# Tap rows among the first fillers, and a filter transpose that hands half of its PSUM banks to the first filter stage

## The chip, the cores and the metric

The kernel runs on one core of one Trainium2 chip. The metric is device time in microseconds for one execution of the whole program; for a set of runs, the median. TensorE, VectorE (DVE), ScalarE (ACT), GpSimd (POOL) and SyncE (SP) each run their own list of instructions in order and wait for each other on semaphores. Transfers are issued from SP and from GpSimd and run on 16 DMA engines.

## What is computed

One block of a sequence model with S = 2048 positions, D = 448 channels and F = 1792 hidden units, all in bfloat16. A mixer part and a part that mixes along the sequence follow each other, each with a layer norm ahead and a residual behind:

```python
k_shift = sum over t of k_pad[:, t:t + S, :] * shift_k[:, ks - 1 - t]   # ks = 4 taps
kv = k_shift * v
y  = irfft(rfft(kv, 2S) * rfft(ssm_k, 2S))[:, :S, :] + kv * ssm_D       # long convolution
h  = x + layernorm(x) * y
u  = gelu(einsum("bsd,sf->bdf", layernorm(layernorm(h)), w1) + b1)
h2 = h + transpose(einsum("bdf,fs->bds", u, w2) + b2)
```

Here x is the input q. The filter ssm_k is D x S: channels come first in memory, so it has to be transposed before it can be treated like kv.

## The kernel before

The sequence is laid out as 128 partitions times R = 16 rows: position 16 q + r is partition q, row r. All work is on rows of 448 channels.

The long convolution is a Fourier transform in two stages, made with matmuls. The first stage multiplies each of the 16 rows by a table E of sines (two matmuls a row, into two PSUM banks), ScalarE copies the pair of banks to a ring in SBUF (L943), and two transfers shuffle it to the layout of the second stage: the larger part from GpSimd's queue, the smaller from SP's (both L947). The ring (`wring`) has 8 buffers, so the copy of a row waits until the shuffle eight rows earlier has landed. The second stage (L964) takes the block table FW. Both stages run once for the filter ("k1", "k2") and once for kv ("u1", "u2"). Products of the two spectra (L1015) and a first inverse stage (L1027) follow, a shuffle back (L1037), a second inverse stage (L1103) with the gate and the statistics of the two layer norms, and then three long runs of matmuls: L1198 and L1208 with w1, L1218 with w2.

Ahead of that stand:

- the loads (`emit_loads`), all on SP's queue: the filter in four blocks of channels (L808, the 64-channel one first), ssm_D (L828), the taps shift_k in one partition (L811), k and v in four pieces each (L816, L825), and last the three rows of k that each partition needs from its neighbour, the halo (L820, L822)
- the tables (`emit_tables`): E from sines on ScalarE (L764), FW and the inverse tables through a chain over GpSimd, VectorE and ScalarE (L771, L775, L777, L779, L788, L791); the table set of the activation functions is changed once (L793)
- the taps (`emit_kv`): a matmul with a row of ones spreads each of the four tap rows to all partitions (L868), and a copy brings it to SBUF. Then, for each row, VectorE multiplies four shifted rows of k by the taps (L879), TensorE adds the four products with an identity (L885), and VectorE multiplies two rows of the sum by v (L888). u1 needs the result
- the filter transpose (`emit_kT`): 64 transposes (L914), for each of 8 groups of two rows and each of 4 blocks of channels, into PSUM, and one copy to SBUF a group
- fillers (`dummy`, L904): matmuls without use, 9 at the start and 3 after some transposes

A copy out of PSUM is written once (`evac`) and goes to ScalarE (L652, with a scale L653) or VectorE (L655, with a scale L656).

The order is not written by hand. Every operation gets a due time `sch.t0`; a list scheduler (`schedule`) takes, for each engine, among the operations that are ready by its cost estimates and that can get their PSUM banks or ring buffers, the one with the earliest due time. The result is a fixed list of instructions for each engine with the waits that the data and the buffers demand. PSUM has 8 banks, given out by the scheduler at the first write and taken back after the last read. The constants T_... and N_... at the top of the build are the due times and the numbers of fillers.

Of the kernel before, what the change touches and what calls it, by code (L numbers as in the profile page):

```python
# [509 lines left out]
def _build(nc, A_q, A_k, A_v, A_shift_k, A_ssm_k, A_ssm_D, B_w1, B_b1, B_w2, B_b2, out):  # L510
# [35 lines left out]
    o_SK = o_WT + 3584  # L546
# [19 lines left out]
    with ctx:  # L566
# [69 lines left out]
            return PS[:, b.slots[i], :].bitcast(dt_)  # L636

        FX = ("act", "dve")
        T_KV, T_DKV, T_KT, T_K1, T_DK1, T_U1, T_DU1 = -37.75, 0.96, -26.42, -39.56, 0.44, 2.72, 0.9
        T_K2, T_U2, T_D2, T_CT, T_BIAS, T_I1, T_DI1 = 29.29, -14.6, 1.375, 22.37, 56.3, 7.01, 0.974  # L640
        T_Q, T_DQ, T_I2, T_DI2, T_M1, T_W1 = 83.98, 14.35, 85.76, 0.401, 102.98, 122.45

        T_TH, T_TN = -36.0, -30.0
        T_CP, T_XL, T_WB = 20.0, -35.53, 154.44
        N_WZ, N_WI, N_W0, N_WK = 34, 6, 9, 3

        def evac(dst, src, w, b, n, scale=None, engs=FX, r=(), est=None):

# [155 lines left out]
        def emit_loads():  # L804
            Dq = "sp"
            for i, c in enumerate((3, 0, 1, 2)):
                sch.t0 = -20.0 + i
                op(Dq, lambda e, W, c=c: e.dma_start(KN[0:CW[c], c, :], A_ssm_k[128 * c:128 * c + CW[c], :]),  # L808
                   w=[(o_KN + 4096 * c, 4096)], dmab=CW[c] * 4096)
            sch.t0 = -15.0  # L810
            op(Dq, lambda e, W: e.dma_start(SK[0:1, :], A_shift_k.rearrange("(a d) j -> a (d j)", a=1)),  # L811
               w=[(o_SK, 3584)], dmab=3584, keng=1)
            op("pool", lambda e, W: e.memset(KH[0:1, 0:3, :], 0.0), w=[(o_KH, 3 * DB, "halo")], n=3 * D)
            for c in range(4):
                sch.t0 = -14.0 + c
                op(Dq, lambda e, W, c=c: e.dma_start(KH[:, 3 + 4 * c:7 + 4 * c, :], k2d[:, 4 * c:4 * c + 4, :]),  # L816
                   w=[(o_KH + (3 + 4 * c) * DB, 4 * DB)], dmab=128 * 4 * DB)
                if c == 3:
                    sch.t0 = -10.5
                    op(Dq, lambda e, W: e.dma_start(KH[1:113, 0:3, :], k2d[0:112, 13:16, :]),  # L820
                       w=[(o_KH, 3 * DB, "halo")], dmab=112 * 3 * DB)
                    op(Dq, lambda e, W: e.dma_start(KH[113:128, 0:3, :], k2d[112:127, 13:16, :]),  # L822
                       w=[(o_KH, 3 * DB, "halo")], dmab=15 * 3 * DB, keng=15)
# [37 lines left out]
        ONE = view(o_one, [128])  # L861

        def emit_kv():
            sch.t0 = -39.0
            op("pool", lambda e, W: e.memset(ONE, 1.0), w=[(o_one, 256)], n=128)
            for j in range(4):
                b = _Buf(psum)
                op("pe", lambda e, W, b=b, j=j: e.matmul(  # L868
                    Pb(b), ONE[0:1, :], SK[0:1, :].rearrange("p (d j) -> p j d", j=4)[:, 3 - j, :], start=True, stop=True),
                   r=[(o_one, 256), (o_SK, 3584)], bw=[b], n=D)  # L870
                evac(lambda j=j: WT[:, j, :], lambda b=b: Pb(b), [(o_WT + j * DB, DB)], b, D)
            for c in range(8):
                sch.t0 = T_KV + T_DKV * c
# [32 lines left out]

        def emit_kT():
            bs = [_Buf(psum) for _ in range(8)]
            for i, c in enumerate((3, 0, 1, 2)):
                for g in range(8):  # L910
                    sch.t0 = T_KT + 0.9 * g
                    for rr in range(2):
                        r = 2 * g + rr
                        k = op("pe", lambda e, W, b=bs[g], rr=rr, r=r, c=c: e.transpose(  # L914
                            out=Pbf(b, 0)[:, rr * D + 128 * c:rr * D + 128 * c + CW[c]],
                            in_=KN[0:CW[c], c, r:S:R], identity=ID[0:CW[c], 0:CW[c]]),
                            r=[(o_KN + 4096 * c, 4096), (o_ID, 256)], bw=[bs[g]], kind="tr")
                    if g == 5 and i < 3:
                        dummy(N_WK, T_KT + 0.9 * g, (k,))
            for g in range(8):  # L920
                sch.t0 = T_KT + 0.9 * g
                evac(lambda g=g: KT[:, 2 * g:2 * g + 2, :].rearrange("p a d -> p (a d)"),
                     lambda b=bs[g]: Pbf(b, 0)[:, 0:2 * D], [(o_KT + 2 * g * DB, 2 * DB)], bs[g], 2 * D,
                     est={"act": 911.0, "dve": 630.0})
# [353 lines left out]
```

## Time and profile before

| | us |
|---|---|
| median of 13 runs | 191.87 |
| lowest and highest run | 189.38, 192.84 |
| the profiled execution | 189.38 |
| its span, first to last instruction | 187.6 |
| busy: TensorE, VectorE, ScalarE, GpSimd | 172.7, 109.3, 97.2, 73.5 |
| first L943 copy starts | 16.47 |
| last inverse shuffle (GpSimd, L1037) is issued | 82.29 |

The span leaves out 1.8 us of the execution around the instructions. A busy TensorE is not TensorE at its peak, and fillers count as busy. The views used below are the page (busy shares in 40 slices and the costliest groups), the chain of waits that ended last, the timeline of one engine (start, duration, engine, line, operation, shapes, count; in brackets the idle time of the engine before it and what ended it), busy time by stretches, and the answers on single lines of the source with the time from a transfer's issue to its landing.

### The profile page before, as it was taken

The page shows a single profiled execution, that of the slowest core. Times are in us where ns is not written, and L with a number is a line of the kernel's source. Part 1 is how long each engine was busy: PE and PEld are TensorE (multiplying, and loading weights), DVE is VectorE, ACT ScalarE, POOL GpSimd, SP SyncE. Part 2 cuts the span into 40 slices and gives each one's busy share as a digit, 9 for nine tenths or more (in the row PEclk, how much of TensorE's full clock was granted, in tenths as well). Part 3 has the DMA queues.
Part 4 walks back from the last instruction along what each step waited for, and adds up shares of the span by engine and source line. Part 5 has one row for each costly group of instructions (what it writes and reads, how often), then busy time and mean ns, then how long its engine had stood idle before and what let it go on. Part 6 is the DMA issues. An engine that isn't in the chain of part 4 may idle for free.

```text
span 187.6 us, 2810 instructions
## 1 busy us (share of the span) xinstructions
PE 172.7 (92%) x1025; PEld 91.2 (49%) x1025; DVE 109.3 (58%) x179; ACT 97.2 (52%) x141; POOL 73.5 (39%) x178
## 2 busy tenths in 40 slices
PE   7998898999997989899599599999999999999993
PEld 2644343434332433244245245455556777777772
DVE  8859799797789999996877874100000222212221
ACT  3487989979889989932984285262121000000000
POOL 8935987698710044485488755100000000000000
PEclk9999999999999999999999999999999999999999
DMA  5998698788649997773999997000000100111111
GB/s 160 365 417 311 171 236 241 211 239 233 193 148 345 388 372 234 223 218 111 380 419 418 414 404 301 7 0 0 0 0 3 49 19 30 49 49 52 49 49 49
DMA packets 15725, 35.44 MB, mean 189 GB/s; under 512 B 3869, under 2 KB 9886, under 8 KB 15710
## 3 DMA queue, kind: packets, MB, share of 16 engines
q1 hardware_dynamic: 11102, 25.59, 36.5%
q0 software_dynamic: 4608, 9.66, 18.0%
q8 instruction: 8, 0.13, 0.3%
q14 instruction: 7, 0.06, 0.1%
HBM read 22.37 MB, written 1.84 MB: 129 GB/s over the span
## 4 chain that ended last, share of the span: by engine, by line
PE 62%; POOL 11%; DMA 9%; ACT 8%; DVE 5%; issue 3%; SPq 1%; POOLq 0%; ACTq 0%
PE ps L1218 23%; PE ps L1208 11%; PE ps L1198 7%; DMA arena<-arena 6%; PE ps L1027 5%; ACT arena L652 4%; PE ps L964 4%; DMA arena<-in_A_ssm_k_dram 3%; PE ps L885 3%; POOL arena L947 3%; PE ps L933 3%; POOL arena L1152 2%; PE ps L914 2%; PE ps L1103 1%; POOL arena L1149 1%
## 5 line engine op out<-in xcount | busy, mean ns | idle before, releaser
L1222 DVE SCALAR_TENSOR_TENSOR arena<-ps,arena 128x448 bf16<-128x448 f32 x16 | 10.9, 684 | 55.2 <-PE ps L1218 55.2
L1218 PE MATMUL ps<-arena 128*128 128x448 bf16 x224 | 42.5, 353 | 0.0
L1218 PEld LDWEIGHTS ps<-arena 128*128 128x128 bf16 x224 | 32.3, 144 | 10.1
L943 ACT CAST arena<-ps 128x896 bf16<-128x896 f32 x32 | 26.7, 931 | 3.5 <-PE ps L937 1.4
L1198 PE MATMUL ps<-arena 128*128 128x448 bf16 x112 | 23.0, 353 | 1.0 <-DVE arena L1158 1.0
L652 ACT CAST arena<-ps 128x896 bf16<-128x896 f32 (+1 forms) x26 | 22.0, 909 | 3.5 <-PE ps L868 2.6
L947 POOL DMA_DIRECT2D arena<-arena x32 | 19.2, 602 | 6.1 <-ACT arena L943 3.4
L1208 PE MATMUL ps<-arena 128*128 128x448 bf16 x112 | 21.5, 353 | 0.0
L964 PE MATMUL ps<-arena 128*64 128x448 bf16 x128 | 16.4, 362 | 1.8 <-ACT arena L652 1.0
L1110 ACT ACTIVATE arena<-ps,arena 128x448 f32<-128x448 f32 x16 | 11.1, 724 | 13.2 <-PE ps L1103 8.5
L1037 POOL DMA_DIRECT2D arena<-arena x16 | 9.4, 594 | 20.8 <-PE ps L964 15.6
L1188 ACT ACTIVATE arena<-ps,arena 128x448 bf16<-128x448 f32 x14 | 8.1, 642 | 18.0 <-PE ps L1208 14.3
L879 DVE TENSOR_TENSOR arena<-arena 128x1792 bf16<-128x1792 bf16 x16 | 17.4, 1122 | 0.0
L933 PE MATMUL ps<-arena 128*128 128x448 bf16 x64 | 16.0, 355 | 1.3 <-ACT arena L943 1.3
L1198 PEld LDWEIGHTS ps<-arena 128*128 128x128 bf16 x112 | 10.9, 98 | 11.7 <-DVE arena L1158 2.0
L1015 DVE TENSOR_TENSOR arena<-arena 128x1792 bf16<-128x1792 bf16 x16 | 16.4, 1085 | 0.0
L1208 PEld LDWEIGHTS ps<-arena 128*128 128x128 bf16 x112 | 11.0, 98 | 10.2
L885 PE MATMUL ps<-arena 128*128 128x448 bf16 x64 | 14.5, 354 | 1.5 <-ACT arena L943 1.4
L1027 PE MATMUL ps<-arena 64*128 64x448 bf16 x128 | 14.1, 352 | 1.3 <-DVE arena L1015 0.6
L1117 DVE SCALAR_TENSOR_TENSOR arena<-arena 128x448 f32<-128x448 bf16 x16 | 10.5, 679 | 4.7 <-ACT arena L1110 4.6
L655 DVE CAST arena<-ps 128x896 bf16<-128x896 f32 (+2 forms) x11 | 9.5, 876 | 2.7 <-PE ps L868 1.2
L964 PEld LDWEIGHTS ps<-arena 128*64 128x64 f16 x128 | 5.4, 108 | 11.4 <-ACT arena L652 4.6
(86 smaller groups left out, 199.1 us busy)
## 6 DMA issues: line engine op xcount, KB each, us to landing
arena<-arena POOLq DMA_DIRECT2D x48, 196.0 KB, 5.7
arena<-in_B_w_dram SPq DMA_DIRECT2D x8, 896.0 KB, 15.4
arena<-in_B_w_dram SPq DMA_DIRECT2D x2, 2048.0 KB, 9.6
arena<-in_B_w_dram SPq DMA_DIRECT2D x2, 1536.0 KB, 17.0
arena<-in_A_k_dram SPq DMA_DIRECT2D x4, 448.0 KB, 8.7
arena<-in_A_v_dram SPq DMA_DIRECT2D x4, 448.0 KB, 9.0
arena<-in_A_q_dram SPq DMA_DIRECT2D x4, 448.0 KB, 5.9
out_dram<-arena SPq DMA_DIRECT2D x7, 224.0 KB, 1.9
```

What stands on the lines that cost most here:

```text
L652: return e.copy(out=dst(), in_=src())
L879: op("dve", lambda e, W, T=T, i=i, r=r: e.tensor_tensor(out=T[:, i], in0=KH[:, r:r + 4, :], in1=WT, op=ALU.mult), r=[(o_KH + r * DB, 4 * D ...
L885: op("pe", lambda e, W, b=b, T=T, i=i, j=j: e.matmul(Pb(b, i), ID, T[:, i, j, :], start=(j == 0), stop=(j == 3)), r=[(o_ID, 256), (o + (i ...
L933: op("pe", lambda e, W, b=b, r=r, h=h, dl=dl: e.matmul(Pb(b, h), E[:, 2 * r + h, :], src[:, r, :], start=True, stop=not dl), r=[r_E(r), (o ...
L943: return e.copy(out=dst, in_=Ppair(b)) if W == "act" else e.tensor_copy(out=dst, in_=Ppair(b))
L947: shuf[tag + q_ + str(r)] = shuf[tag + q_] = op(q_, lambda e, W, w=w, p0=p0, a=a, b_=b_, j0=j0: e.dma_start(T[p0:p0 + 29:4, j0:j0 + (b_ - ...
L964: op("pe", lambda e, W, b=bs[h], h=h, j=j, c=c, par=par: e.matmul(PS[64 * par:64 * par + 64, b.slots[c], 0:D], FW[:, 64 * c:64 * c + 64], ...
L1015: op("dve", lambda e, W, m=m, i=i: e.tensor_tensor(out=MR(m.slots[0]).rearrange("p (x y) d -> p x y d", x=2), in0=TU[:, i].unsqueeze(2).br ...
L1027: k = op("pe", lambda e, W, b=bs[h], m=ms[h], par=par, t=t, tab=tab, xy=xy, P=P: e.matmul(Pb(b, par), tab[P, :], MR(m.slots[0])[P, xy, :], ...
L1198: op("pe", lambda e, W, r=r, fc=fc, b=bs[fc]: e.matmul(Pb(b), W1A[:, r, 128 * fc:128 * fc + 128], Q[:, r, :], start=(r == 0), stop=(r == R ...
L1208: op("pe", lambda e, W, r=r, fc=fc, b=b: e.matmul(Pb(b), W1B[:, r, 128 * (fc - n0):128 * (fc - n0) + 128], Q[:, r, :], start=(r == 0), sto ...
L1218: op("pe", lambda e, W, r=r, fc=fc, b=b: e.matmul(Pb(b), W2[fc // 7][:, fc % 7, r:S:R], G[:, fc, :], start=(fc == 0), stop=(fc == NFC - 1) ...
```

## The change

Four things are edited, all of the opening:

1. The taps' load gets an earlier due time (-25 instead of -15), so that it is the first transfer on SP. The four matmuls that spread the taps get a due time of -62 instead of -39 and an estimate of their own; they come among the fillers that open TensorE's list.
2. The filter transpose walks its groups in two halves. Groups 0 to 3 are transposed block by block as before, as each block of the filter arrives. Groups 4 to 7 follow group by group, with due times between those of the first filter stage, so that four banks are free for that stage before they begin.
3. The first filter stage gets due times that start later and lie further apart.
4. Constants: the due times of u2 and of the products, and fewer fillers (8 instead of 9 at the start, 2 instead of 3 behind transposes).

```diff
-        T_KV, T_DKV, T_KT, T_K1, T_DK1, T_U1, T_DU1 = -37.75, 0.96, -26.42, -39.56, 0.44, 2.72, 0.9
-        T_K2, T_U2, T_D2, T_CT, T_BIAS, T_I1, T_DI1 = 29.29, -14.6, 1.375, 22.37, 56.3, 7.01, 0.974
+        T_KV, T_DKV, T_KT, T_K1, T_DK1, T_U1, T_DU1 = -37.75, 0.96, -45.0, -25.62, 0.72, 2.72, 0.9
+        T_K2, T_U2, T_D2, T_CT, T_BIAS, T_I1, T_DI1 = 29.29, -15.87, 1.375, 22.37, 56.3, -30.85, 0.584
...
-        N_WZ, N_WI, N_W0, N_WK = 34, 6, 9, 3
+        N_WZ, N_WI, N_W0, N_WK = 34, 6, 8, 2
...
-            sch.t0 = -15.0
+            sch.t0 = -25.0
             op(Dq, lambda e, W: e.dma_start(SK[0:1, :], A_shift_k.rearrange("(a d) j -> a (d j)", a=1)),
...
         def emit_kv():
-            sch.t0 = -39.0
+            sch.t0 = -62.0
...
-                   r=[(o_one, 256), (o_SK, 3584)], bw=[b], n=D)
+                   r=[(o_one, 256), (o_SK, 3584)], bw=[b], n=D, est=380.0)
...
             bs = [_Buf(psum) for _ in range(8)]
-            for i, c in enumerate((3, 0, 1, 2)):
-                for g in range(8):
-                    sch.t0 = T_KT + 0.9 * g
-                    for rr in range(2):
-                        r = 2 * g + rr
-                        k = op("pe", lambda e, W, b=bs[g], rr=rr, r=r, c=c: e.transpose(
...
-                    if g == 5 and i < 3:
-                        dummy(N_WK, T_KT + 0.9 * g, (k,))
+            order = [(c, g) for c in (3, 0, 1, 2) for g in range(4)] + [(c, g) for g in range(4, 8) for c in (3, 0, 1, 2)]
+            t_g = [T_KT + 0.9 * g if g < 4 else T_K1 + T_DK1 * (2 * g - 5) for g in range(8)]
+            for i, (c, g) in enumerate(order):
+                sch.t0 = t_g[g]
+                for rr in range(2):
+                    r = 2 * g + rr
+                    k = op("pe", lambda e, W, b=bs[g], rr=rr, r=r, c=c: e.transpose(
...
+                if i in (3, 7, 11):
+                    dummy(N_WK, T_KT + 0.9 * g, (k,))
             for g in range(8):
-                sch.t0 = T_KT + 0.9 * g
+                sch.t0 = t_g[g]
```

What the scheduler makes of it, by the lists of instructions: TensorE's list has 1021 matmuls instead of 1025. It begins with 7 fillers, the four tap matmuls and one more filler. ScalarE copies all four tap rows ahead of the sines. The first row of the first filter stage stands ahead of the last transposes. In GpSimd's list the first shuffle moves ahead of L771. From the middle of the first inverse stage on, the lists of all engines are the same as before. Lines after the change's diff move down by one (L943 becomes L944, and so on); the text before the result uses the numbers of the kernel before.

More of the change, by code (lines that the diff above doesn't have):

```diff
@@ L908, in emit_kT @@
             bs = [_Buf(psum) for _ in range(8)]
-            for i, c in enumerate((3, 0, 1, 2)):
-                for g in range(8):
-                    sch.t0 = T_KT + 0.9 * g
-                    for rr in range(2):
-                        r = 2 * g + rr
[L914 to L917, printed above, removed]
-                    if g == 5 and i < 3:
-                        dummy(N_WK, T_KT + 0.9 * g, (k,))
+            order = [(c, g) for c in (3, 0, 1, 2) for g in range(4)] + [(c, g) for g in range(4, 8) for c in (3, 0, 1, 2)]
[5 more added lines that the diff above has]
+                    k = op("pe", lambda e, W, b=bs[g], rr=rr, r=r, c=c: e.transpose(
+                        out=Pbf(b, 0)[:, rr * D + 128 * c:rr * D + 128 * c + CW[c]],
+                        in_=KN[0:CW[c], c, r:S:R], identity=ID[0:CW[c], 0:CW[c]]),
+                        r=[(o_KN + 4096 * c, 4096), (o_ID, 256)], bw=[bs[g]], kind="tr")
+                if i in (3, 7, 11):
+                    dummy(N_WK, T_KT + 0.9 * g, (k,))
             for g in range(8):
-                sch.t0 = T_KT + 0.9 * g
+                sch.t0 = t_g[g]
                 evac(lambda g=g: KT[:, 2 * g:2 * g + 2, :].rearrange("p a d -> p (a d)"),
```

## The prediction

> **What bounds the kernel now.** I read the chain of waits first, for what sets the end, then the timelines of ScalarE, VectorE, GpSimd and the SP queue over the opening, then busy time by stretch, then single lines for their transfers.
>
> The chain (start, duration, what):
>
> ```profile
> 1.99 5.97 DMA arena<-in_A_ssm_k_dram
> ...
> 13.39 1.53 PE ps L914 x16
> ...
> 16.47 0.91 ACT arena L943
> ...
> 30.98 0.53 ACT L793
> ...
> 33.28 0.93 PE ps L885 x4
> ...
> 82.93 4.56 DMA arena<-arena
> ...
> 142.32 42.39 PE ps L1218 x224
> ```
>
> The end hangs on a TensorE run that is back to back from about 107 to 184.7 us. What feeds it begins with the last shuffle of the inverse (82.93), and that hangs, through two long stages of copies, on the opening: filter load, transposes (L914), first ScalarE copy at 16.47. So a change of the opening counts only as far as it moves 82.93.
>
> ScalarE and VectorE after the opening (start, duration, count, idle before and its releaser):
>
> ```profile
> 16.47 8.19 ACT L943 CAST arena<-ps 128x896 bf16<-128x896 f32 x10 [1.37 <-PE ps L937]
> 30.94 1.28 ACT L793 ACT_TABLE_LOAD   x1
> ...
> 19.89 3.09 DVE L879 TENSOR_TENSOR arena<-arena 128x1792 bf16<-128x1792 bf16 x3
> 36.05 1.09 DVE L888 TENSOR_TENSOR arena<-ps,arena 128x896 bf16<-128x896 f32 x1 [1.12 <-PE ps L885]
> 46.19 1.09 DVE L888 TENSOR_TENSOR arena<-ps,arena 128x896 bf16<-128x896 f32 x1 [0.86 <-PE ps L885]
> ```
>
> VectorE runs the kv chain (15 of 16 L879, all 8 L888) from 19.89 to 47.28: 27.4 us, with four gaps that sum to 2.7 us (0.23, 1.12, 0.53, 0.86). ScalarE copies at 0.80 us start to start beside it.
>
> ```profile
> 12.00:16.50 4.50, 4.50 (x34) 2.48 (x34) 3.69 (x10) 3.13 (x6) 0.52 (x2) 1.00 1.02 416
> 19.90:33.30 13.40, 11.45 (x57) 4.93 (x58) 13.14 (x14) 12.76 (x17) 10.77 (x20) 1.00 0.82 226
> 50.00:80.00 30.00, 26.88 (x240) 10.19 (x238) 27.83 (x28) 27.93 (x34) 9.07 (x20) 1.00 0.82 277
> ```
>
> Columns: stretch, length, busy PE, PEld, DVE, ACT, POOL, clock, DMA share, GB/s. The k and v loads fill the DMA engines before 16.5 (share 1.02). From 19.9 to 33.3 VectorE and ScalarE are both nearly full, and again from 50 to 80.
>
> Why VectorE starts at 19.89:
>
> ```profile
> 8.07 0.45 SPq L820 DMA_DIRECT2D arena<-in_A_k_dram  x1
> ...
> L822 SPq DMA_DIRECT2D arena<-in_A_k_dram x1: 440/440/440, 8.6 to 8.6; - x1
> ...
> DMA to landing us min/median/max: 10.9/10.9/10.9
> ```
>
> The halo rows of k (L820, L822), last in the queue of loads, land at 8.56 + 10.9 = 19.5, and the second L879 in VectorE's order needs them.
>
> **What the Trainium skill says.** "DMA: Bandwidth & Descriptors", section "Queues, rings and completion order": each DMA engine serves the queues in turn, packet by packet, and takes one queue's descriptors in ring order. The trace agrees on the order: the tap load, 3.5 KB, issued at 3.31, was only waited for and met at 9.49, behind the filter blocks. No long stretch of the trace has shuffles against loads, so the sharing is not shown. "TensorE: Matmul & The Clock Gate", Part 1: the array runs at half rate at first and again after an idle window of about 3.4 us. The trace shows the first: nine fillers in 3.54 us, 0.37 us apart, against 0.19 later. "ScalarE: Activation LUTs", "What ACT_TABLE_LOAD costs": about 1283 ns; the trace has 1.28 us.
>
> **The change part by part.**
>
> *Tap load first on SP, taps among the fillers.* L811 takes 0.22 us plus 0.04 on SP, so the four filter loads are issued, and land, 0.26 later; all loads after its old place keep their issue time, but in a full queue they land 0.26 later too. In an empty queue the taps land by 0.73 + 3.6 = 4.3 at the latest (3.6: the first filter load, issue to landing). TensorE has run its 7 fillers by 1.38 + 7 x 0.37 = 4.0, so the taps take about 4.1 to 6.1 (4 x 0.48), where TensorE had nothing else: cost zero. ScalarE now copies all four taps (0.43 each) ahead of the sine tables L764, which start at 6.4 instead of 5.32; the GpSimd copies behind them (L985) end about 1.1 later, covered by GpSimd's idle 4.8 us before L771. If that cover were gone, L771 would move by the 1.1.
>
> *Four fillers fewer* (one of 9, three of 9): 4 x 0.19 to 0.37 us on an engine that waits for loads: zero.
>
> *Transposes.* 64 before and after. Groups 0 to 3 hold four banks; the fourth filter block lands at about 9.3 + 0.26 = 9.5, eight transposes at 0.1 follow, 10.3; VectorE copies (0.53 each; it does seven of the eight, five before, and no taps, all ahead of its wait for the halo), 10.9; row 0 of the first stage on TensorE from 11.1; ScalarE, in its order behind two more pieces of L764 and one copy, starts L943 at 12.2 instead of 16.47: **4.3 us earlier**.
>
> *What is late next.* The L943 copies write a ring of 8 buffers. The ninth waits until the first shuffle out of the ring has landed, its GpSimd part and its SP part. The SP part stands behind all k, v and halo loads in SP's queue. So ScalarE makes eight copies, 12.2 to about 20.6, and stops until the halo has landed. In that wait it also does L779 (0.80) and the table load with its activation (1.4), which the order puts after the sixth and seventh copy.
>
> *What the early shuffles do to the loads.* In GpSimd's new order one shuffle is issued at 13.4, the second behind L771 (16.0), the third and fourth behind L775 (17.5 and 18.1); then L788 and L791 wait for L779 and hold the fifth until 21.8. Four shuffles of 196 KB fall among the loads. Price of one: at least 200.7 KB at 416 GB/s, 0.48 us; at most at the rate of the stage that is nearly all shuffles, 226 GB/s at share 0.82, so 276 GB/s when busy, 0.73 us. I take 0.70, near the top, since the loads have no slack and shuffles move poorly. The halo lands at 19.5 + 0.26 + 4 x 0.70 = 22.5 and VectorE restarts at 22.6: **2.7 us later** (2.2 to 3.2 between the bounds).
>
> *The balance.* At its restart VectorE has 2.7 us less time; ScalarE has more behind it: 8 copies instead of 4.3 by 19.89 (3.7 x 0.80 = 3.0), L779 and the table load (2.2): 5.2 us. From there to the end of the inverse the two engines share the copies out of PSUM (L652/L655, L653/L656), so at best 5.2/2 = 2.6 us comes back; not all, since the kv chain is VectorE's alone and L943 ScalarE's alone. The least that comes back is the gap at 36.05 (1.12, which the chain leads back to the table load) and, by estimate, 0.4 of the other three: 1.5. I take 2.25. Sum: 2.7 - 2.25 = **+0.45 us** (-0.4 at 2.2 less 2.6, +1.7 at 3.2 less 1.5).
>
> *After that* the order of instructions is unchanged: the last 568 on TensorE, 89 on VectorE, 51 on ScalarE are the same in both. The product stage's new due times only reorder u2, k2 and products inside the full stretch, 50 to 80: zero, within 0.4 either way. The shift passes to the end one to one.
>
> Against the profiled execution: 189.38 + 0.45, span 187.6 to 188.05. That execution is the quickest of the runs shown; against the median of 191.87 I get 192.3.
>
> **The rivals.**
>
> *Traded away* (0.60): as above, 192.3. For: DMA share 1.02 while the loads run; the ring.
>
> *Loads starve* (0.20), slower. If the halo's last packets are not in by about 23, when the fifth shuffle starts to move (issued 21.8), the shuffles of four more full buffers go ahead too: 8 x 0.70 instead of 4 x 0.70, halo at 25.3, VectorE 5.5 us late, 5.5 - 2.25 = +3.2: 195.1. TensorE would then stand idle near 3.4 us before L885 and might fall to half rate. For: the margin is half a microsecond. Against: ScalarE's stop itself ends the supply of shuffles.
>
> *Early start kept* (0.12), faster. If loads keep the engines and shuffles take only the leavings, the halo lands near 19.5 + 0.26 + 0.2, VectorE is 0.4 late, and 0.4 - 2.25 = -1.9: 190.0. Against: packets are served in turn, and nothing orders a load first.
>
> *It doesn't start earlier* (0.08). If the taps still wait, or cold fillers push the transposes, L943 starts near 15: two shuffles fall among the loads (+1.4 + 0.26), about 1.6 us of ScalarE work plus 0.8 comes ahead: 1.66 - 1.2, rounded +0.4: 192.3 as well.
>
> **How the numbers follow.** A measurement of this kernel tells about 1% from no change, 1.9 us. Slower by more: the starved case and the upper tail of the first, 0.24. Faster by more: most of the third case and a little of the others, 0.13. Same: 0.63. The range runs from the third case, 189.9, to the second, 195.2; the likeliest case alone spans 191.4 to 193.6.
>
> **What would show it right or wrong.** First L943 near 12.2 (if near 15 or later, the fourth rival); a stop of ScalarE of 1.5 to 3 us after its eighth L943; four GpSimd shuffles issued before 20 us; L820 and L822 landing near 22.5; the second L879 near 22.6; a last L888 ending one to two us after 47.28; L793 before 22. The prediction is wrong if the halo lands before 21 with L943 at 12.2, or after 24, or if the last inverse shuffle, 82.29 now, moves by more than 1.5 us in either direction.

## The result and the profile after

| | before | after |
|---|---|---|
| median of the runs side by side, us | 191.54 (48 runs, 188.47 to 194.33) | 193.96 (11 runs, 192.54 to 194.74) |
| ratio, 95 % interval | | 1.0204 (1.0175 to 1.0233) |
| profiled execution (among the quicker ones of its kernel), its span | 189.38, 187.6 | 192.58, 190.4 |
| end of the last L888 | 47.28 | 50.69 |
| last inverse shuffle starts to move | 82.93 | 85.49 |
| start of the last run of matmuls | 142.32 | 145.13 |

The change makes the kernel 2.0 % slower. The forecast was "no change", 192.3 us; 193.96 lies inside its range, on the side that it gave 0.24, but the way there is another. Ratios here and below compare undisturbed runs only, made in turn with runs of before, so they need not equal the quotient of two medians: here that is 1.013, since before's slower runs, which the ratio leaves out, count in its median.

In the kernel after, and in all quotations of it, lines from the filter transposes on are one higher (L914 is L915, L933 is L934, L943 is L944, L947 is L948, L964 is L965); those ahead, the kv chain, the loads and the tables among them, kept theirs. The chain of waits of after (start, duration, what):

```profile
23.89 2.61 PE ps L885 x8
26.50 0.75 PE ps L934 x2
27.25 2.66 PE ps L885 x12
...
85.49 4.55 DMA arena<-arena
...
145.13 42.39 PE ps L1219 x224
```

The chain no longer begins with the filter load and the transposes. It begins at the first L885, in the kv chain, and comes 2.56 us later to the last inverse shuffle and 2.81 us later to the end run.

ScalarE of after on the timeline, then VectorE (start, duration, count, idle before and its releaser):

```profile
13.23 0.91 ACT L944 CAST arena<-ps 128x896 bf16<-128x896 f32 x1 [0.33 <-PE ps L938]
...
16.90 3.33 ACT L944 CAST arena<-ps 128x896 bf16<-128x896 f32 x4 [1.47 <-PE ps L934]
...
21.55 1.28 ACT L793 ACT_TABLE_LOAD   x1
22.95 3.31 ACT L944 CAST arena<-ps 128x896 bf16<-128x896 f32 x4
...
19.38 3.36 DVE L879 TENSOR_TENSOR arena<-arena 128x1792 bf16<-128x1792 bf16 x3 [0.68 <-DMA arena<-in_A_k_dram]
25.05 1.09 DVE L879 TENSOR_TENSOR arena<-arena 128x1792 bf16<-128x1792 bf16 x1 [2.31 <-PE ps L885]
...
29.19 1.09 DVE L888 TENSOR_TENSOR arena<-ps,arena 128x896 bf16<-128x896 f32 x1 [1.56 <-PE ps L885]
```

VectorE gets its halo on time and runs three L879, then stands 2.31 us for TensorE's L885. ScalarE has two early copies, at 13.23 and 14.53, and then none before 16.90. What both wait for is on TensorE:

```profile
14.33 1.88 PE L915 MATMUL ps<-arena 128*128 128x128 bf16 x19
...
23.89 2.61 PE L885 MATMUL ps<-arena 128*128 128x448 bf16 x8 [1.76 <-ACT arena L944]
```

Row 2 of the first stage, and with it the third copy, stands behind nineteen transposes. The first L885 waits for a copy of ScalarE. That is the eighth, 22.95 to 23.84, and it stands behind the table load. L885 reads nothing that the copies write, so what the copy gives it is the pair of PSUM banks. In before it was the sixth copy (20.46 to 21.43), with only copies between the first and it, and GpSimd issued its second to seventh shuffle in a row:

```profile
21.48 1.69 PE L885 MATMUL ps<-arena 128*128 128x448 bf16 x8 [0.26 <-ACT arena L943]
...
19.51 3.61 POOL L947 DMA_DIRECT2D arena<-arena  x6
```

GpSimd of after, and the halo's transfer:

```profile
18.24 1.26 POOL L948 DMA_DIRECT2D arena<-arena  x2
20.82 2.64 POOL L788 TENSOR_TENSOR arena<-arena 128x128 f16<-128x128 f32 x3 [1.32 <-ACT arena L779]
23.44 0.55 POOL L791 TENSOR_SCALAR arena<-arena 128x128 f16<-128x128 f16 x1
23.95 4.13 POOL L948 DMA_DIRECT2D arena<-arena  x7
...
L822 SPq DMA_DIRECT2D arena<-in_A_k_dram x1: 506/506/506, 8.0 to 8.0; - x1
...
DMA to landing us min/median/max: 11.3/11.3/11.3
```

After four early shuffles GpSimd issues none from 19.5 to 23.95. The halo, issued at 8.03, lands at 19.36; before, it landed at 19.44. The stretch that was nearly full for VectorE and ScalarE (busy PE, PEld, DVE, ACT, POOL, clock, DMA share, GB/s):

```profile
19.90:33.30 13.40, 10.39 (x44) 4.29 (x44) 8.78 (x9) 10.21 (x14) 9.18 (x15) 0.87 0.62 169
```

VectorE does 8.78 us of work here, against 13.14 before: nine instructions for fourteen. The clock is 0.87, since TensorE ran at half rate from 24.51 to 27.92.

### The profile page after: what moved, and what is told of

Its sections match the earlier page's. It is cut to its first block, busy times and chain, and to the rows that moved or that the text cites. A ratio compares the mean times of both kernels' runs of the same rounds, so it can differ in the third digit from the quotient of the medians.

```text
span 190.4 us, 2808 instructions
## 1 busy us (share of the span) xinstructions
PE 175.0 (92%) x1021; PEld 92.0 (48%) x1021; DVE 107.9 (57%) x176; ACT 97.8 (51%) x144; POOL 73.6 (39%) x178
## 4 chain that ended last, share of the span: by engine, by line
PE 52%; DVE 13%; POOL 9%; ACT 6%; issue 3%; DMA 2%; POOLq 0%
PE ps L1219 22%; PE ps L1209 11%; PE ps L885 5%; PE ps L965 4%; DVE arena L1016 4%; PE ps L1028 3%; DVE arena L655 3%; ACT arena L652 3%; POOL arena L1153 3%; PE ps L1199 2%; DMA arena<-arena 2%; PE ps L934 2%; POOL arena L1150 2%; DVE arena L879 2%; ACT arena L944 1%
## 5 line engine op out<-in xcount | busy, mean ns | idle before, releaser
L1219 PE MATMUL ps<-arena 128*128 128x448 bf16 x224 | 42.5, 353 | 0.0
L944 ACT CAST arena<-ps 128x896 bf16<-128x896 f32 x32 | 27.0, 920 | 6.5 <-PE ps L934 5.1
L652 ACT CAST arena<-ps 128x896 bf16<-128x896 f32 (+2 forms) x30 | 23.1, 846 | 3.5 <-PE ps L868 2.5
L1199 PE MATMUL ps<-arena 128*128 128x448 bf16 x112 | 23.0, 353 | 1.1 <-DVE arena L1159 1.1
L948 POOL DMA_DIRECT2D arena<-arena x32 | 19.2, 600 | 11.1 <-ACT arena L944 8.8
L1209 PE MATMUL ps<-arena 128*128 128x448 bf16 x112 | 21.5, 353 | 0.0
L879 DVE TENSOR_TENSOR arena<-arena 128x1792 bf16<-128x1792 bf16 x16 | 17.7, 1140 | 3.0 <-PE ps L885 2.3
L1111 ACT ACTIVATE arena<-ps,arena 128x448 f32<-128x448 f32 x16 | 11.1, 723 | 13.2 <-PE ps L1104 8.5
L965 PE MATMUL ps<-arena 128*64 128x448 bf16 x128 | 16.9, 362 | 1.0 <-ACT arena L944 0.3
L934 PE MATMUL ps<-arena 128*128 128x448 bf16 x64 | 16.1, 362 | 1.7 <-ACT arena L944 1.7
L885 PE MATMUL ps<-arena 128*128 128x448 bf16 x64 | 15.7, 379 | 1.8 <-ACT arena L944 1.8
L1028 PE MATMUL ps<-arena 64*128 64x448 bf16 x128 | 14.6, 352 | 2.0 <-DVE arena L1016 1.0
L965 PEld LDWEIGHTS ps<-arena 128*64 128x64 f16 x128 | 5.7, 108 | 11.7 <-DVE arena L655 2.1
L653 ACT ACTIVATE arena<-ps 128x896 bf16<-128x896 f32 x12 | 10.6, 919 | 1.3 <-PE ps L965 1.3
```

What stands on the lines that cost most here:

```text
L652: return e.copy(out=dst(), in_=src())
L879: op("dve", lambda e, W, T=T, i=i, r=r: e.tensor_tensor(out=T[:, i], in0=KH[:, r:r + 4, :], in1=WT, op=ALU.mult), r=[(o_KH + r * DB, 4 * D ...
L885: op("pe", lambda e, W, b=b, T=T, i=i, j=j: e.matmul(Pb(b, i), ID, T[:, i, j, :], start=(j == 0), stop=(j == 3)), r=[(o_ID, 256), (o + (i ...
L934: op("pe", lambda e, W, b=b, r=r, h=h, dl=dl: e.matmul(Pb(b, h), E[:, 2 * r + h, :], src[:, r, :], start=True, stop=not dl), r=[r_E(r), (o ...
L944: return e.copy(out=dst, in_=Ppair(b)) if W == "act" else e.tensor_copy(out=dst, in_=Ppair(b))
L948: shuf[tag + q_ + str(r)] = shuf[tag + q_] = op(q_, lambda e, W, w=w, p0=p0, a=a, b_=b_, j0=j0: e.dma_start(T[p0:p0 + 29:4, j0:j0 + (b_ - ...
```

## The theories

1. *The bank behind the table load.* The change puts L779 and the table load (L793, 1.28 us and its activation) ahead of ScalarE's eighth copy, and L885 needs the banks that this copy frees.
2. *The half clock.* TensorE is nearly idle ahead of L885, its clock drops for 3.4 us, and this is the loss.
3. *The order on TensorE.* Two rows more stand ahead of the first L885, transposes stand between rows, twelve L885 follow each other; this costs it whatever ScalarE does.
4. *GpSimd's hold* (formed after the first four runs). L788 and L791, waiting for L779, stand ahead of the fifth shuffle. The shuffles behind them are late, and the ring of eight stops ScalarE.

The rival of the forecast, *shuffles hold up the loads*, is answered by the landing above. All kernels that only move instructions do it after the planner, in its finished order, so that everything else keeps its place:

```diff
         order = self.schedule()
+        for what, row in reversed(self.moved):
+            order.remove(what)
+            order.insert(order.index(self.copies[row]) + 1, what)
```

## The experiments

**First four: theories 1 to 3.**

e1_table_late:

```diff
-            op("act", lambda e, W: e.activation(out=JK[:, 0:1], ..., func=ACT.Gelu_apprx_tanh), ...)
+            k = op("act", lambda e, W: e.activation(out=JK[:, 0:1], ..., func=ACT.Gelu_apprx_tanh), ...)
+            sch.moved.append((k, 15))
```

> After with one instruction moved: the activation behind which the table load stands (L793) goes behind the sixteenth filter copy on ScalarE; every other instruction keeps its place. Theory 1 (L885's first PSUM pair is freed by ScalarE's eighth filter copy, which the change put behind L779 and the table load): the eighth copy starts at about 21.5 instead of 22.95, the first L885 at about 22.5 instead of 23.89, the clock window that ends at 24.5 is no longer idle and stays at full rate, the kv chain ends 1.4 to 2.5 us earlier than 50.69, the whole 1.5 to 2.5 us below after, that is within 1 us of before. Theory 3 (the new order of the matmuls on TensorE costs the time, whatever ScalarE does): L885 starts earlier but the chain's end and the whole move by less than 0.5 us. Rival (the shuffles hold up the loads): nothing changes, since the halo is as it was.

Measured: ratio to before 1.0163 (1.0123 to 1.0202). The first L885 came at 22.49, as theory 1 has it, but the last L888 ended at 51.92 and the whole gained at most 0.4 % on after. VectorE and GpSimd of this kernel (its L885 is L879, L894 is L888, L956 the shuffle, L891 the matmul L885):

```profile
25.41 5.31 POOL L956 DMA_DIRECT2D arena<-arena  x9
...
30.88 1.09 DVE L894 TENSOR_TENSOR arena<-ps,arena 128x896 bf16<-128x896 f32 x1 [1.68 <-PE ps L891]
...
36.98 1.09 DVE L894 TENSOR_TENSOR arena<-ps,arena 128x896 bf16<-128x896 f32 x1 [3.01 <-PE ps L891]
```

The two early gaps are gone and two others, 1.68 and 3.01 us, have come. ScalarE stops 2.91 us before its thirteenth copy. What it waits for is seen by setting each copy beside the landing of GpSimd's shuffle eight rows earlier (us; worked out from the trace of each kernel):

| copy | after: copy, shuffle | e1_table_late | e3_before_table_early | e10_before_both_early | e16_after_no_hold |
|---|---|---|---|---|---|
| 13 | 30.33, 27.17 | 28.57, 28.51 | 30.23, 27.85 | 30.39, 28.93 | 27.23, 24.42 |
| 14 | 31.13, 28.63 | 30.07, 30.00 | 31.03, 28.36 | 31.19, 30.40 | 28.03, 25.01 |
| 15 | 31.93, 30.16 | 31.09, 31.07 | 31.82, 29.50 | 31.99, 31.49 | 28.83, 27.24 |
| 16 | 32.72, 31.17 | 32.15, 32.13 | 32.62, 31.22 | 32.78, 32.43 | 29.62, 27.62 |
| 17 | 33.52, 32.65 | 34.86, 34.84 | 33.42, 32.66 | 34.30, 34.23 | 30.42, 30.02 |
| 18 | 34.37, 33.12 | 35.66, 35.03 | 34.22, 32.84 | 35.40, 35.33 | 31.27, 30.20 |

In e1_table_late copies 13 to 17 start 0.02 to 0.07 us after the shuffle lands: the ring stops ScalarE, because the fifth shuffle was not issued before 25.41. This is what led to theory 4.

e2_filled_window:

```diff
+                    def mm(e, W, b=b, r=r, h=h, dl=dl):
+                        for _ in range(10 if tag == "k" and r == 10 and h == 0 else 0):
+                            e.matmul(Pb(b, h), E[:, 2 * r + h, :], src[:, r, :], start=True, stop=True)
+                        return e.matmul(Pb(b, h), E[:, 2 * r + h, :], src[:, r, :], start=True, stop=not dl)
```

> After with ten repeats of one first-stage matmul (row 10, same operands, same bank, same values) put just before the first L885, so that TensorE is busy from about 21.6 to 23.5; everything else keeps its place. Theory 2 (the idle TensorE before L885 drops its clock to half for 3.4 us, and this costs a good part of the loss): clock 1.0 from 24.5 to 27.9, L885 x8 in about 1.7 us instead of 2.61, kv chain about 1.0 to 1.5 us earlier, whole about 1 us below after. Theory 1 alone: the first L885 still starts near 23.9 and the whole moves by 0.3 us at most. Theory 3: clock full, whole unchanged.

Measured: 1.0152 (1.0104 to 1.0200). The ten repeats ran from 22.55 to 24.61, the clock stayed full, and L885 x8 took 1.69 us. It started at 24.86, as soon as the eighth copy ended; the whole opening of this execution was 0.97 us later than in that of after (first copy at 14.21). By these two ratios the half clock is worth half a per cent, and the intervals, which overlap, leave room for nothing and for one. Two executions of after itself speak against it as the main cause: with a mean granted clock of 1.0 they took 194.41 and 194.53 us, while that of the profile, at 0.982, took 192.58. What stands in its place in e2 is told after the sum.

e12_both (the two edits together):

> Both edits: table load behind the sixteenth copy, and ten repeats of row 10's matmul before L885. Theory 1 with theory 2 as a consequence of it: like the first kernel, since without the late copy there is no idle window to fill; at most 0.3 us between the two (the repeats may even delay L885 by 0.5). If both are independent losses: 2.5 to 3.5 us below after, faster than before. Theory 3: within 0.5 us of after.

Measured: 1.0148 (1.0105 to 1.0191), no more than either alone. The repeats held L885 back to 24.64.

e3_before_table_early (before, with L779 and L793 at the change's places):

```diff
+            sch.moved.append((k, 5))
...
+            sch.moved.append((k, 6))
```

(the first stands behind L779 and means behind the sixth copy, the second behind L793, behind the seventh)

> Before with two instructions moved on ScalarE, to the place that the change gives them: L779 behind the sixth filter copy, the activation with the table load (L793) behind the seventh; nothing else is moved. Theory 1: the first L885 starts at 23.5 to 24 instead of 21.48, the kv chain ends 1.5 to 2.5 us later than 47.28, the whole is 1.5 to 2.5 us slower than before, i.e. this move alone makes the loss. Theory 3, or the shuffles against the loads: the whole changes by 0.5 us at most.

Measured: 1.0003 (0.9959 to 1.0047). Theory 1's number was wrong here, and for the first L885 the reason fits its mechanism: in before it waits for the sixth copy, and both instructions stand behind that. L885 came at 22.59, 5.0 us after the first copy (17.58); in before's own trace it was 5.0 as well (16.47 to 21.48). But the second group of L885 does wait, 1.54 us at 26.19, and VectorE behind it 1.51 us. That this costs the whole nothing that can be told from zero is measured; why, no run shows. A wait in a trace is not yet a loss.

**Next four: which part of the change, and theory 4.**

e4_without_tap_move:

```diff
-        N_WZ, N_WI, N_W0, N_WK = 34, 6, 8, 2
+        N_WZ, N_WI, N_W0, N_WK = 34, 6, 9, 2
...
-            sch.t0 = -25.0
+            sch.t0 = -15.0
...
-            sch.t0 = -62.0
+            sch.t0 = -39.0
```

(and the estimate of 380 ns for L868 taken out)

> After with the tap move taken back (tap load at its old place in SP's queue, tap broadcasts between the transposes, nine and two fillers); the split of the transposes and all new due times stay. If the loss comes from the split and the new order (theories 1, 3, 4), this kernel is as slow as after, 193.5 to 194.5 us, ratio 1.010 to 1.018 to before. If it comes from the tap move, it is at before's time, ratio 0.997 to 1.003.

Measured: 1.0375 (1.0318 to 1.0432), outside both expectations. The planner made another order of it further down (no second-stage matmul L965 ahead of the last L885), so it isolates nothing.

e5_tap_move_alone:

```diff
-        N_WZ, N_WI, N_W0, N_WK = 34, 6, 9, 3
+        N_WZ, N_WI, N_W0, N_WK = 34, 6, 8, 3
...
-            sch.t0 = -15.0
+            sch.t0 = -25.0
...
-            sch.t0 = -39.0
+            sch.t0 = -62.0
```

(and the estimate of 380 ns for L868)

> Before with the tap move alone (tap load first on SP, tap broadcasts among the first fillers, one filler fewer at the start); transposes and due times as before. The four taps leave TensorE between 9.5 and 13.4, where the chain of before had them, so the first filter copy may start up to 1.0 us earlier; the kv chain, bound by VectorE and the halo, gains 0.5 us at most: ratio 0.995 to 1.002. If the tap move carries the loss: 1.010 to 1.015.

Measured: 1.0025 (0.9998 to 1.0051). The tap move, with what the planner re-ordered behind it (here too all engines' lists differ from before's in places), costs nothing that can be told from zero.

e6_gpsimd_late:

```diff
-                op("pool", lambda e, W, k=k, dst=dst, i=i: e.tensor_tensor(out=dst, ...))
+                m = op("pool", lambda e, W, k=k, dst=dst, i=i: e.tensor_tensor(out=dst, ...))
+                sch.moved.append((m, "pool11"))
...
+            sch.moved.append((m, "pool11"))
```

(the second for L791; "pool11" is the shuffle of row 11)

> After with L788 (three) and L791 on GpSimd moved behind the twelfth filter shuffle; nothing else is moved. Theory 4 (the change puts them, waiting for L779, ahead of the fifth shuffle, so that GpSimd issues no shuffle from 19.5 to 23.95; the ring of eight then stops ScalarE and through its PSUM pairs TensorE's L885): fifth shuffle issued at about 20 instead of 23.95, the gaps before the twelfth and thirteenth filter copies (1.07 and 2.09 us) shrink to under 1 us together, the last L888 about 1 us earlier than 50.69, whole 0.5 to 1.5 us below after; the rest of the loss stays because the table load still stands before the eighth copy. Theory 3 (the order of the matmuls alone): within 0.4 us of after.

Measured: 1.0185 (1.0151 to 1.0220), no gain. I had read the gap before the thirteenth copy as the ring's; it stayed (1.58 us, releaser TensorE's row matmul behind twelve L885). Its lines (L892 is the matmul L885, L886 is L879, L793 is L788, L797 is L791):

```profile
25.15 1.69 PE L892 MATMUL ps<-arena 128*128 128x448 bf16 x8 [1.76 <-ACT arena L951]
...
26.12 1.09 DVE L886 TENSOR_TENSOR arena<-arena 128x1792 bf16<-128x1792 bf16 x1 [3.16 <-PE ps L892]
...
29.23 2.14 POOL L793 TENSOR_TENSOR arena<-arena 128x128 f16<-128x128 f32 x3
31.35 1.37 POOL L797 TENSOR_SCALAR arena<-arena 128x128 f16<-128x128 f16 x1
32.69 4.71 POOL L955 DMA_DIRECT2D arena<-arena  x8
```

The table load still holds L885, and the hold was not taken away but moved: four small instructions in a row keep GpSimd from 29.23 to 32.69, and copies 22 to 26 start 0.02 to 0.07 us after a shuffle lands. That became clear only with e8 and e16.

e7_gpsimd_and_table_late (both edits):

> Both: L788 and L791 behind the twelfth shuffle on GpSimd, and the table load behind the sixteenth copy on ScalarE. Theory 4 with theory 1: each edit alone only hands the wait over to the other, both together free ScalarE, so the first L885 at about 22.5, no stop of ScalarE before the thirteenth copy (3.1 us in the run with the table load late alone), last L888 at 48 to 49.5, whole 2 to 3 us below after: ratio 0.995 to 1.004 to before. Theory 3: ratio 1.010 to 1.018.

Measured: 1.0065 (1.0039 to 1.0091), a little above the expected band, and the first kernel to take back most of the loss: 1.4 of 2.0 %. Each edit alone had hardly moved it. L885 came at 23.19 and no copy waited for a shuffle; VectorE now stood 1.43 us behind the table load's new place.

**Then: the converse, and other places.**

e8_after_table_idle (as e7, but the table load just before the first L1111, where ScalarE waits for the last inverse shuffle; the waits of other engines for the table load are taken out):

```diff
+        order.remove(self.table)
...
+        order.insert(next(k for k, i in enumerate(order) if i in self.gates and self.ops[i].eng == "act"), self.table)
```

> After with L788 and L791 behind the twelfth shuffle, as in the run before, and the table load not in the kv stage at all but just before the first L1111, where ScalarE waits some 6 us for the last inverse shuffle. Theory 4 with theory 1 (ScalarE and GpSimd hand waits to each other): the gap of VectorE before its fourth L888 (1.43 us behind the table load in the run with both late) goes, last L888 near 48.5 to 49, whole 0.5 to 1.2 us below the run with both late: ratio to before 0.998 to 1.005. If the table load in the kv stage costs nothing by now: 1.004 to 1.009 as there.

Measured: 1.0069 (1.0047 to 1.0091), the same as e7. The gap behind the table load is gone, and the whole did not gain: the four moved instructions keep GpSimd from 27.43 to 30.88, and copies 22 to 26 start 0.02 to 0.07 us after a shuffle lands.

e9_before_table_idle:

> Before with the table load alone moved to ScalarE's wait for the last inverse shuffle; nothing else moves. The gap of VectorE before its fifth L888 (1.12 us, which the chain of before leads back to the table load) should go: 0.5 to 1.1 us below before, ratio 0.994 to 0.998. If before's ScalarE has slack there: 0.998 to 1.002.

Measured: 1.0017 (0.9988 to 1.0046). The gap that before's chain leads to the table load was slack.

e10_before_both_early (before, with L779, L793, L788 and L791 all where the change has them; nothing of its split):

```diff
+            sch.moved.append((k, 5))
...
+                sch.moved.append((m, 5))
...
+            sch.moved.append((m, 5))
...
+            sch.moved.append((k, 6))
```

(in this order L779, the three L788, L791 and L793; the shuffles from the fifth on follow behind L791)

> The converse, before with all of the change's order on these two engines and nothing of its split: on ScalarE L779 behind the sixth filter copy and the table load behind the seventh, on GpSimd L788 (three) and L791 ahead of the fifth shuffle. Moving the two on ScalarE alone made no difference. Theory 4 with theory 1: GpSimd issues no shuffle for about 5 us and the ring stops ScalarE, so slower by 1.5 to 3 us, ratio 1.008 to 1.015. Theory 3 (the matmul order and the split cost it): 0.998 to 1.003.

Measured: 1.0221 (1.0163 to 1.0279). The order of six instructions on two engines makes the whole loss in a kernel that has no split transposes and no early copy. Its GpSimd (L802 is L788, L806 is L791):

```profile
23.28 2.09 POOL L802 TENSOR_TENSOR arena<-arena 128x128 f16<-128x128 f32 x3 [0.74 <-ACT arena L792]
25.36 0.56 POOL L806 TENSOR_SCALAR arena<-arena 128x128 f16<-128x128 f16 x1
25.88 2.40 POOL L966 DMA_DIRECT2D arena<-arena  x4
```

The fifth shuffle goes out at 25.88, 3.5 us later than in e3, which differs by these four instructions. In the table above, copies 17 and 18 then start 0.07 us after their shuffles; in e3 they have 0.76 and 1.38 to spare.

e11_before_both_late:

> Before with the same two edits as in the first kernel of this call: L788 and L791 behind the twelfth shuffle, the table load in ScalarE's wait for the last inverse shuffle. Against that kernel it shows what the change itself is worth once neither stands in the way: if the residual of the change is its order of matmuls (two more rows ahead of the first L885, twelve L885 in a row), this kernel is faster than it by 0.5 to 1.2 us, ratio to before 0.992 to 0.998. If nothing of the change is left: equal within 0.3 us.

Measured: 1.0020 (0.9989 to 1.0051). It is below e8 (0.5 %, the intervals touch), so something of the change was left.

**The last of the loss.**

e13_kv_before_row8 and e14_kv_before_row9:

```diff
                        r=[r_E(r), (o_src + r * DB, DB)], bw=[b], n=D,
+                       safter=sch.kv[0:1] if tag == "k" and r >= 8 else ())
```

(in the second, `r >= 9`)

> The kernel with L788 and L791 behind the twelfth shuffle and the table load in ScalarE's long wait, and in addition the rows of the first filter stage from row 8 on are planned behind the first kv chunk on TensorE (VectorE's order of L879 and L888 becomes that of before: three, one, one, one, two, one, two). If the residual is this order: first L885 at about 21.5 to 22 instead of 23.35, last L888 about 1 to 1.5 us earlier, ratio to before 0.994 to 1.001. If the residual is in the split or in the stages after it: 1.004 to 1.009, as without this edit. The planner re-orders some product work behind it too, which may add 0.5 us either way.

> The same with the rows from row 9 on behind the first kv chunk: one row more ahead of it, so L885 about 0.8 us later than in the kernel before this one. If the residual is the order of rows and chunks: ratio to before between that one's and 1.006. Otherwise 1.004 to 1.009.

Measured: 1.0103 (1.0079 to 1.0127) and 1.0165 (1.0103 to 1.0228), both slower. In e13 the first L885 did come at 21.59, but the planner re-ordered what follows, and the last L888 still ended at 49.78; in e14 it ended at 48.38, and the loss came behind it. As tests of the order they are inconclusive.

e15_before_hold_alone (as e10, but the table load at before's place):

> Before with L779 behind the sixth filter copy and L788 (three) and L791 on GpSimd ahead of the fifth shuffle, but the table load at its old place behind the sixteenth copy. If GpSimd's hold makes the loss by itself (the ring stops ScalarE): ratio to before 1.008 to 1.022, close to the kernel with the table load early as well. If both are needed (each hides in the other's slack): 0.999 to 1.006.

Measured: 1.0087 (1.0050 to 1.0124). The hold makes a loss by itself; with the table load early as well (e10) it is more than twice that, though the early table load alone (e3) made none. In before the two waits together cost more than the sum of both.

e16_after_no_hold (as e8, but only the L788 that makes FW behind the twelfth shuffle; the other two and L791, which the inverse needs, behind the last):

```diff
-                sch.moved.append((m, "pool11"))
+                sch.moved.append((m, "pool31" if k else "pool11"))
...
-            sch.moved.append((m, "pool11"))
+            sch.moved.append((m, "pool31"))
```

> The kernel with the table load in ScalarE's long wait, and of the four small GpSimd instructions only the one that the kv stage's matmuls need (L788 for FW) behind the twelfth shuffle; the other two L788 and L791, which only the inverse needs, behind the last filter shuffle. Nothing else moves. If the residual of 0.65 % is the second hold of GpSimd (27.4 to 30.9, then copies 24 to 26 wait for shuffles): the thirteenth shuffle at about 29 instead of 30.88, those waits gone, last L888 0.5 to 1 us earlier, ratio to before 0.998 to 1.004. If it is in the order of TensorE (twelve L885 in a row, two rows more ahead of the first): 1.004 to 1.009 as before this edit.

Measured: 1.0000 (0.9974 to 1.0025). The residual was the second hold, which my own edit had made. TensorE's order in this kernel is that of after, word for word, so theory 3 falls. GpSimd and VectorE of it (L799 is L788, L963 the shuffle, L892 is L879, L901 is L888):

```profile
26.55 0.47 POOL L799 TENSOR_TENSOR arena<-arena 128x128 f16<-128x128 f32 x1
28.43 0.63 POOL L963 DMA_DIRECT2D arena<-arena  x1 [1.41 <-ACT arena L957]
...
23.45 1.09 DVE L892 TENSOR_TENSOR arena<-arena 128x1792 bf16<-128x1792 bf16 x1 [1.00 <-PE ps L898]
```

The thirteenth shuffle goes out at 28.43 as soon as its copy is there, and the last L888 ends at 47.60, 3.1 us before that of after.

e17_before_no_hold:

> Before with the same edits: table load in ScalarE's long wait, L788 for FW behind the twelfth shuffle, the other two and L791 behind the last. Before has no such hold (its L788 stand one by one in gaps), so it stays where it was: 0.998 to 1.003.

Measured: 0.9984 (0.9951 to 1.0018). Before had no hold to lose. No kernel of the study is faster than before by more than its interval.

e18_after_table_alone (as e16, with the table load where the change put it):

> After with L788 for FW behind the twelfth shuffle and the other two L788 and L791 behind the last one, as in the kernel without any hold; the table load stays where the change put it, ahead of the eighth copy. If the table load there makes a loss of its own (the first L885 at 23.9 or later instead of 22.5): ratio to before 1.006 to 1.014. If all of the loss is GpSimd's hold: 0.998 to 1.004.

Measured: 1.0101 (1.0036 to 1.0165). Its TensorE and VectorE (L892 is the matmul L885, L886 is L879):

```profile
23.98 1.69 PE L892 MATMUL ps<-arena 128*128 128x448 bf16 x8 [1.76 <-ACT arena L951]
...
24.95 1.09 DVE L886 TENSOR_TENSOR arena<-arena 128x1792 bf16<-128x1792 bf16 x1 [1.75 <-PE ps L892]
```

L885 waits 1.76 us for ScalarE, as in after, and the last L888 ends at 49.09, 1.5 us later than in e16: theory 1, now with nothing to cover it.

**The sum.** In the changed kernel:

| | table load late | table load early |
|---|---|---|
| no hold on GpSimd | 1.0000 (e16) | 1.0101 (e18) |
| hold on GpSimd | 1.0163 (e1) | 1.0204 (after) |

The table load costs about 1.0 % without the hold; beside the hold it is 0.4 %, which the intervals don't tell from zero. The hold costs about 1.6 % without the early table load and 1.0 % with it, the latter by intervals that just clear each other (1.0165 and 1.0175). The medians of the four kernels, 190.67 and 192.66 us above, 194.00 and 193.96 below, give each wait alone its loss and the table load none beside the hold. The traces of e1 and e16 agree: they open alike (first copy at 13.33 and 13.32, L885 at 22.49 and 22.48), and the last L888 ends 4.3 us later in e1. Its table load stands behind the sixteenth copy and not in the long wait, but the seventeenth copy starts as its shuffle lands, so the load is not seen to cost there. The rest of the change (tap move, split transposes, early copies, new order on TensorE) is worth nothing that can be told from zero.

How the hold costs time beside the early table load is not seen in the one trace of after: no copy waits for the ring (the smallest margin is 0.34 us), and the 1.6 us between its last L888 and that of e18 come in with the half clock, between L888 at 26.54 and at 29.19. The trace of e2, with the same hold and table load and a full clock, shows one way. Counted from the first copy, VectorE's first five L888 come as in e18 (the fifth at 24.0 us in both); the sixth is 1.1 us behind it and the last 1.4:

```profile
36.61 2.62 ACT L947 CAST arena<-ps 128x896 bf16<-128x896 f32 x3 [0.29 <-DMA arena<-arena]
40.44 0.91 ACT L947 CAST arena<-ps 128x896 bf16<-128x896 f32 x1 [1.22 <-DMA arena<-arena]
...
41.40 0.55 PE L937 MATMUL ps<-arena 128*128 128x448 bf16 x2 [0.90 <-ACT arena L947]
...
42.75 1.09 DVE L888 TENSOR_TENSOR arena<-ps,arena 128x896 bf16<-128x896 f32 x1 [1.44 <-PE ps L885]
```

ScalarE waits for transfers out of the ring, TensorE for ScalarE's banks, VectorE for TensorE; in e18 the same L888 waits 0.39 us. So in these two executions the half clock and the ring stand in for each other, which is a reading of one trace each: with its rows late by the half clock, after no longer meets the ring. What stays open is how the other executions of after divide between the two, and so the 1.0 % rests on the comparison of runs.

## Why the prediction was wrong, step by step

- *Tap load and taps: zero.* Right. The four L868 ran from 4.10 to 5.83, and e5 gives 1.0025 (0.9998 to 1.0051).
- *First copy at 12.2, 4.3 us earlier.* It came at 13.23, 3.2 us earlier. The clock was at half rate from 7.44 to 10.85, with transposes under way.
- *Eight early copies, to about 20.6.* Wrong. Only two kept the lead. Row 2's matmuls stand behind nineteen transposes of the second half (14.33 to 16.2), so the third copy came at 16.90, 1.2 us ahead of before's (18.07), and the eighth at 22.95, 0.9 us behind before's (22.05). The "follows row by row" of the change holds for its first two rows only. The working did not follow TensorE's list past row 1.
- *L779 and the table load fall into the stop of ScalarE.* Wrong, and the first of the two steps that decided it. There is no stop after the eighth copy. The two stand ahead of it, and it frees L885's banks. I priced the ring that the copies write, and not the PSUM banks that they read: the wait for the banks stood at nothing. Measured: L885 waits 1.76 us (0.26 in before), and 1.0 % of the whole in e18.
- *Four shuffles out before GpSimd's hold, the fifth held to 21.8.* The order was right, with issues at 14.44, 16.63, 18.24 and 18.91; the fifth went out at 23.95. I used the hold only to count what falls among the loads, and never asked who waits for the shuffles behind it: that wait stood at nothing too. Second deciding step: 1.0 to 1.6 %.
- *Each early shuffle delays the halo by 0.70 us, 2.8 in all.* Wrong; about zero. The later of the landings of L820 and L822 lies at 19.6 on average over eleven traces with four early shuffles, and at 19.4 over seven without (e4, re-ordered by the planner, and e15, whose trace has a clock of 0.75, not counted). The 0.26 for the tap load alone would make that. The bounds on this price (0.48 to 0.73) were drawn from rates, and neither asked whether the loads yield at all; a lower bound of zero belonged there, and the *early start kept* rival did state it.
- *2.25 us come back from the balance.* Wrong. Nothing came back, since VectorE, with its halo in time, waited 2.31 and 1.56 us for L885.
- *The shift passes to the end one to one.* Nearly: 3.4 us at the last L888, 2.6 at the last inverse shuffle, 2.8 at the end run.
- *The rivals.* "Loads starve" gave 195.1 and the right side, by a mechanism that did not happen. Its remark on an idle TensorE and the half clock came true, from another cause. "Early start kept" had the loads right, but its gain of 2.25 us is not there even in e16, where both waits are out of the way: it is at before's time.
- *The sum.* Its three terms were +2.7 for the halo, -2.25 for the balance and nothing for the two waits; the runs show about zero, nothing and a loss of 2.0 % of 191.5, 3.9 us (2.4 by the two medians).

## What to carry to other kernels

When a plan is re-ordered, ask of every instruction that now stands behind another on its engine which buffers it frees (PSUM banks that it reads as much as ring buffers), and who waits for them. Small instructions with a far deadline, such as a table load or the last steps of a table, belong behind those that free buffers, and one by one into gaps, since four in a row are a hold. Where two waits cover each other, taking away either shows little, so test them together as well as one by one.

## What I had not expected of the hardware

- Loads ahead of shuffles. "DMA: Bandwidth & Descriptors", section "Queues, rings and completion order", of the Trainium skill says that each DMA engine serves its queues in turn. From that I expected four shuffles of 196 KB to take their share from SP's queue of loads. Here the first of them took 5.9 us (issued 14.44, landed 20.34, after the halo's 19.36), against 3.3 for the first shuffle of before (17.68 to 20.97), while the loads lost next to nothing. The measurement decides; why the shuffles yield, no run here shows.
- The clock's phase moves the opening. "TensorE: Matmul & The Clock Gate", Part 1, of the Trainium skill says that the window of 3.4 us runs freely. The half-rate stretches here fit that: they last 3.41 us and begin at different times. In five of the seven traces with before's opening (e11 fell back to half rate in it, e15 was at 0.75) the clock went to full at 4.94, 5.44, 6.75, 10.52 and 10.71 us, and the first filter copy came at 15.57, 16.73, 16.47, 17.74 and 17.58: about 2 us between executions of the same instructions, which is of the order of the effect studied here. And the same gap of 1.76 us before L885 dropped the clock in after (24.51 to 27.92) and not in e6 or e18. One trace against one trace would have misled; the ratios did not.
